# Four small edits to the attention stage: low-rank copies moved on ScalarE, more blank products, V earlier, and scores of two batches as 128-column products

## The chip, the core and the metric

The kernel runs on one core of a Trainium2 chip. A core has five engines that run side by side: TensorE (PE) for matrix products, with its weight loads listed apart as PEld; VectorE (DVE), ScalarE (ACT) and GpSimd (POOL) for elementwise work; and SyncE (SP), which here only issues DMAs. Products write to PSUM, which has banks of 128 rows by 512 fp32 numbers; everything else that is computed lies in SBUF. The metric is the device time of one execution in microseconds, and the kernel before takes 678.25 us (median of 4 runs, 676.69 to 679.31).

## What is computed

A linear attention block with decay feeds a channel mixer with a low-rank token mixing in front. Batch 4, 8 heads, 768 positions, head size 64.

```python
for b in range(nb):                        # blocks of positions
    intra = einsum('bhic,bhjc->bhij', qb, kb) * Dmask      # decay lam^(i-j), j <= i
    intra = einsum('bhij,bhjd->bhid', intra, vb)
    inter = einsum('bhid,bhde->bhie', qb * lam_pow, kv_state)
    out[:, :, sl] = intra + inter
    kv_state = lam_block * kv_state + einsum('bhsd,bhse->bhde', kb * rev_pow, vb)
x = out as (B, S, H*D)                     # 4 x 768 x 512
h = x^T @ U @ V                            # rank 32, over the positions
u = x + h^T
out = u + relu(u @ w_ch1) @ w_ch2          # 512 -> 2048 -> 512
```

U, V, w_ch1 and w_ch2 arrive as 64-bit floats and are turned into fp32 on the chip.

## The kernel before

The attention is cut into 24 steps s of 128 positions, six to a batch. One step has these pieces, each a function of s. `prep` turns q and k of the step with four PE transposes each (L344, banks pq and pk, copied to SBUF by ACT at L347 as qt and kt). `scores` multiplies kt by qt into the two banks pss (L389): for each pair of heads a and each of its two heads x (64 rows of the array each) two products of 64 columns, so 16 products. `masked` multiplies them by the decay mask on DVE (L398, tile sm). `inter` is the carried state's part (L430) and `intra` the step's own (L442); both add into the banks px, which ACT copies to x_nat (L447). `state` makes the new carried state: the product pkv (L407, in the bank pk) and its sum with the faded old state on DVE (L413, L415, tile kv; `fade` on ACT, L381). POOL scales q and k (L372, L361).

An fp32 product shows in the trace as two passes, so 16 products are 32 matmuls and 32 weight loads.

After a batch's six steps `low` multiplies x by U (L457, result pp in the bank of pq), and `low_rows` cuts pp into a high part and a rest: four masks on DVE (L470, tile p_h), two copies of the high part to four-way stacked rows on ACT (L473 h, L474 h2), four differences on DVE (L476, l), and a copy of l on POOL (L479, l2). `mix` multiplies these rows by V's rows v_hl and adds the result to x (L484, L487); `turn` transposes the sum u for the mixer's first product (L501 to L525). p_hl and v_hl lie in one tile, which the profile calls vp.

The order is written out by hand: the list `pieces` (L531 to L547) says which piece follows which, and each engine gets its instructions in that order and runs them in that order. In a step s the pieces are prep(s+1), scale(s+1), then at a batch's first step mix, low and low_rows of the batch before, then intra(s), late, state(s), scores(s+1), inter(s+1), masked(s+1), fade(s+1), aside, turn.

`aside(s)` runs small steps of converting U, V and w_ch1, as the lists at L604 to L608 place them; what they need of ACT is kept back and issued by `late` after the next intra. For V the ten steps are two loads, four conversion steps, the mask with the first two ACT copies (`five`, L576), the difference for one row group on DVE, the last two ACT copies, and the difference for the last row group on POOL. Their places are 0, 0, 3, 3, 4, 4, 5, 5, 5, 5, so that all four ACT copies (L585) come out behind intra of s = 6.

At the start `keep_busy(n)` (L326) issues n products of zeros: one before the product pl, which spreads lam over the rows (L643), and two after it. The first step's q and k are loaded and turned in two halves.

After the attention come the mixer's first product (`hidden`, L695 and L705, whose first units also take the last batch's low, low_rows, mix and turn, by the list `rest` at L749) and its second (`product`, L826 to L830).

Of the kernel before, what the change touches and what calls it, by code (L numbers as in the profile page):

```python
# [8 lines left out]
FP32 = mybir.dt.float32  # L9
# [5 lines left out]
P = 128  # L15
# [3 lines left out]
def kernel(  # L19
# [27 lines left out]
    nc = tc.nc  # L47
# [3 lines left out]
    NT = S // P  # L51
    C = H * D
# [25 lines left out]
    late = []  # L78

    def on_scalar(what):  # L80
        if late and late[0] is None:
            late.append(what)
        else:
            what()
# [12 lines left out]
    def tmp(name):  # L97
        return wconv.tile([P, C], FP32, tag="tmp", bufs=3, name=name)
# [121 lines left out]
    def w1_steps(ft, in_parts=False):  # L220
        def tile_of():
            w1v[ft] = w1_pool.tile([P, 3, C], F32R, tag="w1", name="w1")
            return w1v[ft]

        cols = moe_w_ch1[:, ft * P : (ft + 1) * P].rearrange("(c p) f -> p c f", p=P)
        return split_steps(tile_of, cols, in_parts)
# [13 lines left out]
    def two_banks(name, tag):  # L240
        return psf.tile([P, 2, N], FP32, tag=tag, name=name)

    def one_bank(shape, name, tag):
        return psf.tile(shape, FP32, tag=tag, name=name)
# [11 lines left out]
    def parts(s):  # L256
        return 2 if s == 0 else 1
# [60 lines left out]

    xs = {}
    st = {}
    kv = {}
    half = [slice(0, D), slice(D, P)]

    def keep_busy(n, cols=P):  # L326

        out = one_bank([P, C], "idle", "pq")
        for i in range(n):
            nc.tensor.matmul(  # L330
                out=out[:, 0:cols], lhsT=blank, rhs=blank[:, 0:cols], start=True, stop=True
            )

    qts, kts = {}, {}

    def turn_half(s, a0, name):

        ts, tag = (qts, ("pq", "pt")) if name == "q" else (kts, ("pk", "pu"))
        if a0 == 0:
            ts[s] = att.tile([P, HP, P], FP32, tag=name + "t", bufs=2, name=name + "t")  # L340
        n = HP // parts(s)
        pt = one_bank([P, n, P], "p" + name, tag[a0 > 0])
        for a in range(a0, a0 + n):
            nc.tensor.transpose(  # L344
                out=pt[:, a - a0, :], in_=raw[s, name][:, 2 * a : 2 * a + 2, :], identity=ident
            )
        nc.scalar.copy(ts[s][:, a0 : a0 + n, :], pt)  # L347

    def prep(s):
        for a0 in range(0, HP, HP // parts(s)):  # L350
            for name in "qk":
                turn_half(s, a0, name)
        st[s].update(qt=qts.pop(s), kt=kts.pop(s))
        for name in "qk":
            load_next(name)
# [27 lines left out]
    def scores(s):  # L383
        qt, kt = st[s]["qt"], st[s]["kt"]
        st[s]["pss"] = pss = two_banks("pss", "pss").rearrange("p x (a i) -> p x a i", a=HP)
        for a in range(HP):
            for x in range(2):
                for t in range(2):
                    nc.tensor.matmul(  # L389
                        out=pss[half[t], x, a, :], lhsT=kt[half[x], a, half[t]],  # L390
                        rhs=qt[half[x], a, :], start=True, stop=True,
                    )

# [56 lines left out]
    pps = {}  # L450
# [13 lines left out]
    def low_rows(b):  # L464

        pp, t = pps.pop(b), tmp("p_h")[0:R]
        h, h2, l, l2 = (p_hl[g * R : (g + 1) * R] for g in range(G))
        own = [(slice(g * R, (g + 1) * R), slice(g * P, (g + 1) * P)) for g in range(G)]
        for rows, cols in own:
            nc.vector.tensor_scalar(  # L470
                t[:, cols].bitcast(U32), pp[rows].bitcast(U32), HI, None, ALU.bitwise_and
            )
        nc.scalar.copy(h, t)  # L473
        nc.scalar.copy(h2, t)  # L474
        for rows, cols in own:
            nc.vector.tensor_tensor(  # L476
                out=l[:, cols], in0=pp[rows], in1=t[:, cols], op=ALU.subtract
            )
        nc.gpsimd.tensor_copy(out=l2, in_=l.bitcast(FP32))  # L479

    def mix(s):
        b, c = divmod(s, NT)
# [49 lines left out]
    for s in range(NS):  # L532
        b, c = divmod(s, NT)
        done = s - NT - 1
        more = s + 1 < NS
        step = [("prep", s + 1), ("scale", s + 1)] * more
        step += [("mix", done)] * (0 <= done < NS - NT - 1)
        step += [("low", b - 1)] * (c == 0 and b > 0)
        step += [("low_rows", b - 1)] * (c == 0 and b > 0)
        step += [("intra", s)] + [("late", s)] * (done < 0) + [("state", s)]  # L540
        step += [("turned", done - 1)] * (done > 0) + [("late", s)] * (done >= 0)
        step += [("scores", s + 1)] * more
        step += [("aside", s)] * (done >= 0)
        step += [("inter", s + 1), ("masked", s + 1), ("fade", s + 1)] * more
        step += [("aside", s)] * (done < 0)
        step += [("turn", done)] * (done >= 0 and done // TG < FG)
        pieces += step  # L547
    waiting = {name: list(range(NS)) for name in "qkv"}

    def load_next(name, engine=nc.sync):  # L550
        if waiting[name]:
            load(name, waiting[name].pop(0), engine)


    run = {
        "prep": prep, "fade": fade, "scores": scores, "masked": masked, "inter": inter,
        "intra": intra, "state": state,
        "low": low, "low_rows": low_rows, "mix": mix, "turn": turn,
        "scale": scale, "turned": lambda s: turned.pop(s)(),
    }  # L560
    def v_steps():

        st = {}

        def dst():
            if "v" not in st:
                st["v"] = wconv.tile([P, C], FP32, tag="wf", name="vf")[0 : 2 * R, 0:SH]
            return st["v"]

        def parts(gs):  # L570
            for half in range(2):
                rows, cols = slice(half * R, (half + 1) * R), slice(half * SH, (half + 1) * SH)
                for g in gs:
                    yield v_hl[g * R : (g + 1) * R, cols], rows

        def five():  # L576
            st["t"] = t = wconv.tile([P, C], FP32, tag="wt", name="vt")[0 : 2 * R, 0:SH]
            nc.vector.tensor_scalar(
                t.bitcast(U32), st["v"].bitcast(U32), HI, None, ALU.bitwise_and
            )  # L580
            on_scalar(lambda: high(0))

        def high(g):
            for out, rows in parts((g,)):
                nc.scalar.copy(out, st["t"][rows])  # L585

        def low(g, engine):
            for out, rows in parts((g,)):
                engine.tensor_tensor(
                    out=out, in0=st["v"][rows], in1=st["t"][rows], op=ALU.subtract  # L590
                )

        halves = [moe_V[:, half * SH : (half + 1) * SH] for half in range(2)]
        return weight_steps(dst, halves, SH, 2 * R, in_parts=True) + [
            five, lambda: low(1, nc.vector), lambda: on_scalar(lambda: high(2)),
            lambda: low(3, nc.gpsimd),
        ]
# [5 lines left out]
    side = {}  # L603
    for steps, at in (  # L604
        (u_side, (-1, 1, 1, 2, 2)),
        (v_steps(), (0, 0, 3, 3, 4, 4, 5, 5, 5, 5)),
        (w1_steps(0, True), (3, 4, 5, 6, 8, 9, 10, 11, 12, 13, 14)),
        (w1_steps(1, True), (8, 9, 10, 11, 15, 16, 17, 18, 19, 20, 21)),  # L608
    ):
        assert len(steps) == len(at)  # L610
        for step, n in zip(steps, at):
            side.setdefault(n, []).append(step)
# [15 lines left out]
    blank = x_pool.tile([P, C], FP32, tag="x", name="blank")[:, 0:P]  # L628
# [9 lines left out]
    for name in "qkv":  # L638
        load_next(name)
    make_identity(nc, ident)  # L640
    keep_busy(1)
    pl = one_bank([P, H], "pl", "pt")
    nc.tensor.matmul(out=pl, lhsT=lam_row[:, H:], rhs=lam_row[:, 0:H], start=True, stop=True)  # L643
    keep_busy(2)
    nc.vector.tensor_copy(out=lamb, in_=pl)
    constants()
    powers()
# [92 lines left out]
    def run_units(units, side, every=lambda i: None):  # L740
# [7 lines left out]
    c0, b = NS - NT, B - 1  # L748
    rest = [  # L749
        (0, 4, "enter", None),  # L750
        (0, 4, "turn", c0 - 2), (0, 6, "mix", c0 - 1), (0, 9, "low", b), (0, 14, "low_rows", b),
        (0, 18, "turn", c0 - 1), (0, 22, "mix", c0),
    ]

# [174 lines left out]
```

## Time and profile before

| what | value |
|---|---|
| median of 4 runs | 678.25 us (676.69 to 679.31) |
| profiled execution | 679.33 us, span 677.3 us |
| PE busy | 665.0 us, 98% of the span |
| DVE, ACT, POOL busy | 498.7, 291.6, 116.4 us |
| attention | from 0 to about 125 us |
| first product of the mixer | about 125 to 402 us |
| second product | about 402 to 677 us |
| DMA share, 0 to 44.9 us | 0.90 to 0.96 |

The span runs from the first to the last instruction of the profiled execution. PE's busy share is that of matmuls which are pipelined, with modelled ends. In a row of the timeline a bracket gives the idle time before an instruction and what ended it; "issue" means that the profile shows nothing it waited for. Where several waits end close together, the engine named is the one that came last by the records, and need not be the cause. The mixer's two products run almost without a hole on PE, so the places to look at are those before about 155 us.

### The profile page before, as it was taken

The page shows a single profiled execution, that of the slowest core. Times are in us where ns is not written, and L with a number is a line of the kernel's source. Part 1 is how long each engine was busy: PE and PEld are TensorE (multiplying, and loading weights), DVE is VectorE, ACT ScalarE, POOL GpSimd, SP SyncE. Part 2 cuts the span into 40 slices and gives each one's busy share as a digit, 9 for nine tenths or more (in the row PEclk, how much of TensorE's full clock was granted, in tenths as well). Part 3 has the DMA queues.
Part 4 walks back from the last instruction along what each step waited for, and adds up shares of the span by engine and source line. Part 5 has one row for each costly group of instructions (what it writes and reads, how often), then busy time and mean ns, then how long its engine had stood idle before and what let it go on. Part 6 is the DMA issues. An engine that isn't in the chain of part 4 may idle for free.

```text
span 677.3 us, 13604 instructions
## 1 busy us (share of the span) xinstructions
PE 665.0 (98%) x5312; PEld 543.7 (80%) x5312; DVE 498.7 (74%) x877; ACT 291.6 (43%) x543; POOL 116.4 (17%) x96
## 2 busy tenths in 40 slices
PE   9989999999999999999999999999999999999997
PEld 7878888878888888888888888888888888888885
DVE  4679999776999777777798256786586775865864
ACT  4667768644666444444465131232232322322320
POOL 4456767431000000000000000030030200300300
PEclk9999999999999999999999999999999999999999
DMA  9899894154677655555566999844353363453521
GB/s 214 206 226 227 209 233 129 60 200 161 234 261 254 235 204 201 206 203 203 203 248 252 325 320 388 300 161 162 96 202 109 109 202 94 153 158 93 162 87 63
DMA packets 131777, 131.30 MB, mean 194 GB/s; under 512 B 81346, under 2 KB 89794, under 8 KB 131714
## 3 DMA queue, kind: packets, MB, share of 16 engines
q1 hardware_dynamic: 130656, 130.18, 60.6%
q8 instruction: 42, 0.69, 0.4%
q10 hardware_dynamic: 1058, 0.26, 0.2%
q14 instruction: 21, 0.17, 0.1%
HBM read 80.09 MB, written 50.33 MB: 193 GB/s over the span
## 4 chain that ended last, share of the span: by engine, by line
PE 94%; ACT 2%; DVE 1%; issue 1%; DMA 1%; POOL 0%; ACTq 0%; DVEq 0%
PE pz L695 27%; PE pz L826 13%; PE pz L828 13%; PE pd L705 13%; PE pd L830 13%; PE pss L389 3%; PE px L442 3%; PE put L501 2%; PE pq L344 1%; PE px L430 1%; PE pk L344 1%; PE pkv L407 1%; PE pu L484 1%; PE pp L457 1%; DMA kraw<-in_k_dram 1%
## 5 line engine op out<-in xcount | busy, mean ns | idle before, releaser
L695 PE MATMUL pz<-u_hl,w 128*128 128x512 f32 x768 | 190.7, 398 | 0.2 <-ACT r L701 0.2
L695 PEld LDWEIGHTS pz<-u_hl,w 128*128 128x128 f32 x768 | 143.9, 188 | 35.8 <-ACT r L701 0.9
L826 PE MATMUL pz<-w_hl,m 128*128 128x512 f32 x384 | 151.6, 396 | 0.0
L828 PE MATMUL pz<-w_hl,m 128*128 128x512 f32 x384 | 151.6, 396 | 0.0
L830 PE MATMUL pd<-w_d,m 128*128 128x512 f32 x384 | 150.0, 396 | 0.0
L809 ACT ACTIVATE m<-mt 128x512 fp32r<-128x512 f32 x96 | 60.7, 632 | 195.6 <-PE pd L830 144.5
L810 DVE SCALAR_TENSOR_TENSOR m<-rm,m 128x512 fp32r<-128x512 f32 x96 | 71.5, 746 | 54.1 <-ACT m L809 53.8
L855 POOL TENSOR_TENSOR o<-o,u 128x512 f32<-128x512 f32 x20 | 29.9, 1524 | 447.4 <-DVE o L851 447.4
L710 DVE SCALAR_TENSOR_TENSOR r<-pd,r 128x512 f32<-128x512 f32 x96 | 61.8, 686 | 55.9 <-ACT r L701 45.5
L705 PE MATMUL pd<-u_d,w 128*128 128x512 f32 x384 | 98.2, 397 | 0.0
L826 PEld LDWEIGHTS pz<-w_hl,m 128*128 128x128 f32 x384 | 72.3, 188 | 17.6
L828 PEld LDWEIGHTS pz<-w_hl,m 128*128 128x128 f32 x384 | 72.3, 188 | 17.7
L830 PEld LDWEIGHTS pd<-w_d,m 128*128 128x128 f32 x384 | 72.3, 188 | 17.6
L705 PEld LDWEIGHTS pd<-u_d,w 128*128 128x128 f32 x384 | 72.2, 188 | 17.4
L701 ACT ACTIVATE r<-pz 128x512 f32<-128x512 f32 x96 | 52.0, 593 | 59.1 <-PE pz L695 59.1
L811 DVE SCALAR_TENSOR_TENSOR m<-m 128x512 fp32r<-128x512 f32 x96 | 69.1, 721 | 0.9
L808 DVE TENSOR_SCALAR mt<-rm 128x512 uint32<-128x512 uint32 x96 | 46.1, 481 | 25.1 <-DMA rm<-r_d 24.8
L204 ACT CAST w<-wt 128x512 fp32r<-128x512 f32 x32 | 19.9, 622 | 40.9 <-DVE wt L201 33.7
L398 DVE TENSOR_TENSOR sm<-pss,mask 128x512 f32<-128x512 f32 x48 | 30.8, 682 | 8.0 <-PE pss L389 7.8
L159 ACT ACTIVATE sc<-sc,ends 128x512 f32<-128x512 uint32 x30 | 21.7, 723 | 18.4 <-DVE sc L153 18.4
L372 POOL TENSOR_TENSOR qs<-qt,powq 128x512 f32<-128x512 f32 x20 | 25.8, 1288 | 21.6 <-ACT qt L347 18.6
L442 PEld LDWEIGHTS px<-vraw,sm 128*64 128x64 f32 x768 | 24.5, 138 | 6.0 <-DVE sm L398 2.3
(83 smaller groups left out, 710.6 us busy)
## 6 DMA issues: line engine op xcount, KB each, us to landing
r_d<-r SPq DMA_DIRECT2D x96, 256.0 KB, 2.6
rm<-r_d SPq DMA_DIRECT2D x96, 256.0 KB, 2.7
words<-in_moe_w_ch_dram SPq DMA_DIRECT2D x30, 512.0 KB, 4.5
w_d<-w SPq DMA_DIRECT2D x16, 768.0 KB, 3.3
w_hl<-w_d SPq DMA_DIRECT2D x16, 512.0 KB, 6.2
vraw<-in_v_dram SPq DMA_DIRECT2D x24, 256.0 KB, 4.5
u_d<-x_nat SPq DMA_DIRECT2D x24, 256.0 KB, 3.6
u<-u_d SPq DMA_DIRECT2D x24, 256.0 KB, 4.1
```

Source lines behind the costliest of these rows:

```text
L442: nc.tensor.matmul(out=px[half[t], x, a, :], lhsT=sm[:, x, a, half[t]], rhs=vr[:, 2 * a + x, :], start=(first and a == 0), stop=(a == HP - 1),
L695: nc.tensor.matmul(out=acc[g][0], lhsT=w[:, n, ct, :], rhs=uhl[g][:, n, ct, :], start=(ct == 0 and n == 0), stop=(ct == CT - 1 and n == 1),)
L701: nc.scalar.mul(rs[g], acc[g][0], 1.0 + E)
L705: nc.tensor.matmul(out=acc[g][1], lhsT=w[:, 2, ct, :], rhs=ud[g][:, ct, :], start=(ct == 0), stop=(ct == CT - 1),)
L710: nc.vector.scalar_tensor_tensor(rs[g], acc[g][1], 4096.0, rs[g], ALU.mult, ALU.add)
L808: nc.vector.tensor_scalar(t.bitcast(U32), r.bitcast(U32), HI, None, ALU.bitwise_and)
L809: nc.scalar.activation(out=m[:, 0], in_=t, func=AF.Relu)
L810: nc.vector.scalar_tensor_tensor(m[:, 1], r, 0.0, hi, ALU.max, ALU.subtract)
L811: nc.vector.scalar_tensor_tensor(m[:, 2], hi, E, low, ALU.mult, ALU.subtract)
L826: nc.tensor.matmul(out=pz, lhsT=m[:, 0, cols], rhs=hl[:, 0], start=first, stop=False)
L828: nc.tensor.matmul(out=pz, lhsT=m[:, 1, cols], rhs=hl[:, 1], start=False, stop=end)
L830: nc.tensor.matmul(out=pd, lhsT=m[:, 2, cols], rhs=dd, start=first, stop=end)
```

## The change

Four edits, all in the attention stage and the code around it.

Blank products: `keep_busy` gets two before pl instead of one, three after it instead of two, and the first step gets one behind each half of q, written to the banks pss.

Scores: for s below 12 (the first two batches) one product with 128 columns of kt takes the place of two with 64; for later steps nothing changes.

Low-rank rows: the copies h and h2 leave `low_rows` and come in a piece of their own, `spread`, behind intra (and so behind x's copy); l2 is copied there too, on ACT instead of POOL. In the last batch `spread` follows `low_rows` directly.

V: the mask and all four ACT copies are placed with step 4 instead of 5, so that the copies come out behind intra of s = 5.

```diff
-    def keep_busy(n, cols=P):
+    def keep_busy(n, tag="pq"):
-        out = one_bank([P, C], "idle", "pq")
+        out = one_bank([P, C], "idle", tag) if tag == "pq" else two_banks("idle", tag)[:, 0]
         for i in range(n):
-            nc.tensor.matmul(
-                out=out[:, 0:cols], lhsT=blank, rhs=blank[:, 0:cols], start=True, stop=True
-            )
+            nc.tensor.matmul(out=out[:, 0:P], lhsT=blank, rhs=blank, start=True, stop=True)
...
                 turn_half(s, a0, name)
+                if s == 0 and name == "q":
+                    keep_busy(1, "pss")
...
             for x in range(2):
-                for t in range(2):
+                for rows in half if s >= 2 * NT else [slice(0, P)]:
                     nc.tensor.matmul(
-                        out=pss[half[t], x, a, :], lhsT=kt[half[x], a, half[t]],
+                        out=pss[rows, x, a, :], lhsT=kt[half[x], a, rows],
                         rhs=qt[half[x], a, :], start=True, stop=True,
                     )
...
-        nc.scalar.copy(h, t)
-        nc.scalar.copy(h2, t)
         for rows, cols in own:
             nc.vector.tensor_tensor(
                 out=l[:, cols], in0=pp[rows], in1=t[:, cols], op=ALU.subtract
             )
-        nc.gpsimd.tensor_copy(out=l2, in_=l.bitcast(FP32))
+
+        def spread():
+            nc.scalar.copy(h, t)
+            nc.scalar.copy(h2, t)
+            nc.scalar.copy(l2, l.bitcast(FP32))
+
+        pps[b] = spread
...
-        step += [("intra", s)] + [("late", s)] * (done < 0) + [("state", s)]
+        step += [("intra", s)]
+        step += [("spread", b - 1)] * (c == 0 and b > 0)
+        step += [("late", s)] * (done < 0) + [("state", s)]
...
-        (v_steps(), (0, 0, 3, 3, 4, 4, 5, 5, 5, 5)),
+        (v_steps(), (0, 0, 3, 3, 4, 4, 4, 5, 4, 5)),
...
-    keep_busy(1)
+    keep_busy(2)
     pl = one_bank([P, H], "pl", "pt")
     nc.tensor.matmul(out=pl, lhsT=lam_row[:, H:], rhs=lam_row[:, 0:H], start=True, stop=True)
-    keep_busy(2)
+    keep_busy(3)
...
         (0, 4, "turn", c0 - 2), (0, 6, "mix", c0 - 1), (0, 9, "low", b), (0, 14, "low_rows", b),
+        (0, 14, "spread", b),
```

More of the change, by code (lines that the diff above doesn't have):

```diff
@@ L557 @@
         "intra": intra, "state": state,
-        "low": low, "low_rows": low_rows, "mix": mix, "turn": turn,
+        "low": low, "low_rows": low_rows, "spread": lambda b: pps.pop(b)(), "mix": mix, "turn": turn,
         "scale": scale, "turned": lambda s: turned.pop(s)(),
```

## The prediction

> **What bounds the kernel now.** I read the page's busy shares, then the table of windows, then the timeline wherever TensorE (PE) idles.
>
> ```profile
> PE 665.0 (98%) x5312; PEld 543.7 (80%) x5312; DVE 498.7 (74%) x877; ACT 291.6 (43%) x543; POOL 116.4 (17%) x96
> 9.90:27.90 18.00, 18.00 (x532) 16.66 (x533) 9.81 (x20) 12.59 (x32) 9.59 (x8) 1.00 0.96 220
> 27.90:44.90 17.00, 13.25 (x347) 11.37 (x345) 11.07 (x23) 9.85 (x22) 8.24 (x9) 1.00 0.91 211
> 155.00:402.00 247.00, 247.00 (x1056) 198.55 (x1055) 188.74 (x337) 121.93 (x213) 1.19 (x1) 1.00 0.67 231
> ```
>
> A window's row has its length, the busy time of PE, weight loads, DVE, ACT and POOL, the granted clock, DMA share and GB/s. From 155 us on PE has hardly a hole and the change touches nothing, so a PE that gets there earlier ends the kernel earlier, one for one. Before that PE's holes sum to 6.7 us (from 5.5 us on), 3.75 of them in 27.9 to 44.9.
>
> ```profile
> 6.12 1.99 PE L389 MATMUL pss<-qt,kt 64*64 64x128 f32 x32
> 11.37 1.10 PE L389 MATMUL pss<-qt,kt 64*64 64x128 f32 x32
> 29.75 0.76 PE L389 MATMUL pss<-qt,kt 64*64 64x128 f32 x17 [1.25 <-issue]
> ```
>
> The timeline's columns are start, length, engine, line. The first scores take 1.99 us, the next 1.10: the PE clock opens late; the granted-clock record begins at 9.66 us. At 28.5 us PE stops for 1.25 us inside one stage, where the program has no wait. Packets of the instruction queue (16 KB, 256 instructions) start 0.8 to 1.1 us after PE enters a block at 11.9, 16.3 and 20.5 us, but the one due at 24.8 starts at 27.34. I read the stop as late code, behind loads that keep the DMA engines 96% busy.
>
> ```profile
> 35.54 1.52 PE L457 MATMUL pp<-x_nat,u_w 128*32 128x128 f32 x48 [0.29 <-ACT qt L347]
> 40.27 0.58 ACT L447 COPY x_nat<-px 128x512 f32<-128x512 f32 x1
> 40.75 2.08 ACT L585 CAST vp<-vt 32x384 fp32r<-32x384 f32 x4
> 40.95 0.69 PE L430 MATMUL px<-kv,qs 64*64 64x64 f32 x32 [1.31 <-POOL ks L361]
> 44.28 0.58 ACT L347 COPY kt<-pk 128x512 f32<-128x512 f32 x1
> 44.91 0.69 PE L407 MATMUL pkv<-vraw,ks 128*64 128x64 f32 x16 [0.91 <-ACT kt L347]
> ```
>
> Between the first and second batch ACT is late. The carried-state product (L430) starts 0.07 us after x's copy ends (40.85), which frees its bank px; POOL, the engine named, only ended at the same moment. V's four copies then hold ACT for 2.08 us, kt comes late, and the state product waits 0.91 us for the bank pk.
>
> ```profile
> 72.58 0.42 DVE L413 COPY kv<-pkv 128x256 f32<-128x256 f32 x1
> 72.63 0.58 ACT L447 COPY x_nat<-px 128x512 f32<-128x512 f32 x1
> 73.32 0.30 PE L430 MATMUL px<-kv,qs 64*64 64x64 f32 x5 [0.83 <-POOL vp L479]
> ```
>
> One batch later it is the same, and kv is nearly as late (73.00) as x (73.21).
>
> ```profile
> 85.55 1.01 PEld L442 LDWEIGHTS px<-vraw,sm 128*64 128x64 f32 x32 [0.24 <-DVE ut L506]
> 86.48 0.55 PEld L407 LDWEIGHTS pkv<-vraw,ks 128*64 128x64 f32 x16
> 87.10 0.86 PEld L389 LDWEIGHTS pss<-qt,kt 64*64 64x64 f32 x32
> 87.92 0.61 PEld L430 LDWEIGHTS px<-kv,qs 64*64 64x64 f32 x32
> 88.60 0.20 PEld L501 LDWEIGHTS put<-ident,x_nat 128*128 128x128 f32 x2
> ```
>
> A plain step costs PE start to start: intra 0.93, state 0.62, scores 0.82, inter 0.68 us.
>
> **The change part by part.**
>
> *Blank products, 4 more* (one before pl, one after, one behind each half of q at s = 0). Cold, a 128-column pass takes 0.21 us (two q transposes 3.87 to 4.32 are 0.44) and an fp32 product has two, so each blank costs 0.43. The first ends as lam lands (PE waits 0.20 for it at 2.05), the second fills the hole before q (3.84). The two behind q are on PE's path: k's second half lands at 5.45 and would be turned from 6.0 instead of 5.50, scores start some 0.5 later. Against that, the clock. With blanks until 6.0 I let it open one recording window sooner. Then scores(0) run 6.4 to 7.4, its masking waits for DVE's powers (7.22) and for the scores, prep(1) ends by 8.35, and the first intra starts near 8.8 instead of 9.82: -1.0. If it opens at 9.66 all the same: +0.5. Nearest rows: 1.99 against 1.10 for scores. Behind it loads could bind: q(2) lands at 11.66, 1.2 us ahead of its use at 12.87, so 1.0 still fits. I take -1.0.
>
> The skill's "TensorE: Matmul & The Clock Gate" (Part 1) says that the gate's window runs free of the kernel, so the opening moves from run to run. This trace shows one opening only. By the rule some runs open early already, and half of it, -0.5, would be left in a median.
>
> *Scores in 128-column products, s = 0 to 11* (the condition keeps halves for s >= 12). Per step 8 products instead of 16: 16 fewer passes and 16 fewer loads, 32 of some 240 instructions. Array time: the 32 passes of 64*64 start in fours every 109 ns (8 x 0.109 = 0.87). With 64 rows x 128 columns two tiles fit, 16 passes in twos: 8 x 0.109 again, if the two row halves overlap. No row shows this shape; inter (64*64, four at once) shows that row halves do overlap, the transposes (128*128, one per 109 ns) that whole-array passes don't. Bounds per step: 0 and +0.87. I take 0, since inter shares the row split. What is added for sure is a change of shape between scores and inter in 10 steps. Nearest row: state (128*64) to scores (64*64) opens with 0.10 to 0.15 us more than the passes before it follow each other. Bounds: 0 and 10 x 0.15 = +1.5. In batch 0 intra is released by DVE's masking (26.23, PE at 26.30), which hides most of it, and batch 1 has holes behind two of its five; without these covers it would be +1.5. I charge three steps, +0.3.
>
> The skill's "TensorEngine Tiling (Array Packing)", Key Properties, speaks against this edit: changing the tiling mode, not just the tile, drains the engine. By it all ten steps pay, and the sum below would be 1.2 worse.
>
> *Late code.* A block lasts 256 of 208 instead of 256 of 240 instructions, 0.6 us more at 4.07 us a step. The stop of 1.25 ends between 0 and 1.25 shorter; a block that is consumed 0.6 later also meets another queue. I take -1.25. If a packet is late elsewhere, up to +1.25.
>
> *V sooner.* The mask (DVE, 0.34) goes ahead of masked(6), where DVE is idle (33.0 to 34.29). The four ACT copies go behind x's copy of s = 5, 33.8 to 35.9. Behind them wait qt(7) and kt(7): 36.46 and 36.95 instead of 35.49 and 35.97; the low-rank product needs qt's bank, so its wait grows by 0.97, and intra(6) starts at 38.0 instead of 36.99. But p_h on DVE waited until 37.73 for V's low part anyway, so it slips by 0.3, kv(7) ends at 40.98, inter(7) starts at 41.04 (+0.1). With ACT then free kt(8) ends at 43.7, and the state product follows intra at 43.9 instead of 44.91: -1.0. If qt(7) slips further it is 0.
>
> *Low-rank copies.* On ACT, h and h2 (0.62 each) go behind x, and l2 (0.60 on POOL) joins them as 0.62. POOL's other work stands in the same order and has room. At 72: x ends at 71.6, inter can start at kv + 0.06 = 73.06, -0.25; but te, hi, faded, qt(14), kt(14) slip by 0.4 and the next state product waits until 76.6, where it stood at 76.56. So 0 at both such places (without l2 it would be -0.25 each), and its gain at 41 is in the line above. In the fourth batch l2 ends at 133.5, before pu's 133.66; r (L701) slips 0.6 behind it, hidden by pd products until 134.2, +0.6 if not.
>
> SP issues the same DMAs in the same order.
>
> *Sum:* -1.0 + 0.3 - 1.25 - 1.0 = -2.95 against the profiled 679.33 us (span 677.3 and 2.0 around it): **676.4 us**. That execution is 1.1 above the median of 678.25, so against the median it is -1.85, or -0.27%.
>
> **The rivals.**
> *The code stops are worth more.* The median's own runs spread from 676.69 to 679.31, as stops of 1 to 2.5 us that come and go would make them; seven more code packets fall in batch 1, where the DMA engines are 91 to 92% busy. If the change ends these too, and no shape change shows: 2 us less, 674.4. Against it: this trace has one stop only.
> *The gains are in the best runs already.* Clock early, no stop in half of before's runs, and shape changes paid: V's -1.0, half the clock -0.5, +1.5 less the stop's half -0.6: 677.7.
> *Slower: row halves don't overlap.* Scores then take 16 x 0.109 = 1.74 instead of 0.87 in 12 steps on PE's path: +10.4, 686.8. For it: no row has 64 x 128. It decides against the others once a score stage is over about 1.15 us instead of 0.82 (12 x 0.33 = 3.9, to 0.3% above the median).
> *Slower by lateness:* the blanks delay k and the clock stays (+0.5 for -1.0), qt(7) holds the low-rank product and V gains nothing: 676.4 + 1.5 + 1.0 + 1.2 for the shape changes = 680.1, and some more if the stop stays.
>
> **How the numbers follow.** Forecast 0.45 (own range 675.0 to 677.8, 0.27 of it under 676.2); more code stops ended 0.25; gains present already 0.10; row halves 0.12; lateness 0.08, counted slower with the stop. A measurement of this kernel tells about 0.3% (2.0 us) from no change. Faster by that: 0.27 + 0.25 = 0.52; within: 0.18 + 0.10 = 0.28; slower: 0.20. The range leaves out the row halves and the tail of the first rival: 674.0 to 681.2.
>
> **What would show it.** The granted clock starting near 6.3 and scores(0) at 1.1 us, or not; scores of s < 12 at 0.82 us start to start (1.7 for the rival); inter 0.1 to 0.15 later behind them; no hole marked issue before 45 us; the hole before L457 grown to 1.3 and that before L407 gone; x's copy straight behind intra at 71 us, kv releasing inter. I am wrong if a score stage or a qt copy has become what PE waits for.

## The result and the profile after

The changed kernel takes 677.54 us (median of 52 runs, 676.67 to 678.79) beside 678.89 for the kernel before on the same chip (78 runs, 675.92 to 681.25). The ratio is 0.9982, with an interval of 0.9977 to 0.9988: faster, but by 0.18%, inside the 0.3% that I had set as the bound of a measurable change. Its profiled execution took 677.97 us, span 676.2; the one before took 679.33. The two profiles differ by 1.36 us, the two medians by 1.35, so the profiles can be compared step by step. (Of the 1.36, 1.14 lie in the span, 677.3 to 676.2; the rest lies outside it.)

The page's busy shares, and two rows of the table of windows (length, busy time and instructions of PE, weight loads, DVE, ACT, POOL, granted clock, DMA share, GB/s):

```profile
PE 667.0 (99%) x5128; PEld 545.8 (81%) x5128; DVE 496.5 (73%) x877; ACT 294.1 (43%) x547; POOL 113.4 (17%) x92
9.90:27.90 18.00, 17.90 (x428) 15.91 (x427) 9.32 (x21) 12.06 (x32) 8.28 (x7) 1.00 1.01 228
27.90:44.90 17.00, 15.31 (x367) 13.66 (x363) 10.88 (x25) 11.95 (x25) 9.61 (x9) 1.00 0.98 232
```

PE has 184 instructions fewer, and yet 2.0 us more of busy time. Between 27.9 and 44.9 us it is busy for 15.31 instead of 13.25 us, since holes have closed. What follows is the start of intra(s), the pace of the kernel, read from the timelines of both:

| intra of step | before, us | after, us | after minus before |
|---|---|---|---|
| 0 | 9.82 | 10.16 | +0.34 |
| 1 | 13.89 | 14.77 | +0.88 |
| 4 | 26.30 | 27.64 | +1.34 |
| 5 | 32.03 | 31.93 | -0.10 |
| 6 | 36.99 | 37.79 | +0.80 |
| 8 | 48.72 | 47.88 | -0.84 |
| 12 | 69.83 | 69.10 | -0.73 |
| 15 | 85.55 | 84.33 | -1.22 |
| 23 | 124.30 | 123.02 | -1.28 |

The kernel loses 1.3 us up to step 4, wins it back in step 4 alone, loses 0.9, wins 1.6, and is 1.2 to 1.3 us ahead from step 15 on. The timeline of after (start, length, engine, line, operation, tiles) has the first loss and a plain step of batch 0, one in which PE has no hole:

```profile
7.20 2.00 PE L390 MATMUL pss<-qt,kt 64*128 64x128 f32 x16
...
10.16 1.47 PE L443 MATMUL px<-vraw,sm 128*64 128x64 f32 x32
...
23.35 1.15 PE L443 MATMUL px<-vraw,sm 128*64 128x64 f32 x32
24.33 0.64 PE L408 MATMUL pkv<-vraw,ks 128*64 128x64 f32 x16
24.89 1.16 PE L390 MATMUL pss<-qt,kt 64*128 64x128 f32 x16
25.99 0.69 PE L431 MATMUL px<-kv,qs 64*64 64x64 f32 x32
26.61 0.66 PE L343 MATMUL pq<-ident,qraw 128*128 128x128 f32 x4
```

The first scores start 1.08 us later than before and still take 2.00 us: the blanks delayed them and the clock was not yet open. From score start to inter start it is now 1.10 us (before 0.93), from there to the transposes 0.62 (before 0.57): the plain step grew from 4.07 to 4.29 us. The same stages in the timeline of before:

```profile
23.77 1.10 PE L389 MATMUL pss<-qt,kt 64*64 64x128 f32 x32
24.70 0.64 PE L430 MATMUL px<-kv,qs 64*64 64x64 f32 x32
25.27 0.66 PE L344 MATMUL pq<-ident,qraw 128*128 128x128 f32 x4
```

Single score passes of after start in pairs every 112 ns, so the two row halves do run at once. The stop of 1.25 us with issue as its reason is gone; no PE hole of after has that reason. The change of batches:

```profile
33.61 2.07 ACT L592 CAST vp<-vt 32x384 fp32r<-32x384 f32 x4
35.70 0.58 ACT L346 COPY qt<-pq 128x512 f32<-128x512 f32 x1
36.34 1.52 PE L458 MATMUL pp<-x_nat,u_w 128*32 128x128 f32 x48 [1.15 <-ACT qt L346]
40.47 0.42 DVE L414 COPY kv<-pkv 128x256 f32<-128x256 f32 x1
41.04 0.69 PE L431 MATMUL px<-kv,qs 64*64 64x64 f32 x32 [0.54 <-DVE kv L414]
43.91 0.64 PE L408 MATMUL pkv<-vraw,ks 128*64 128x64 f32 x16
```

V's copies now stand ahead of qt: the low-rank product waits 1.15 us instead of 0.29, inter 0.54 instead of 1.31, and the state product no longer 0.91.

### The profile page after: what moved, and what is told of

The parts are those of the page before. It is cut to its first block, busy times and chain, and to the rows that moved or that the text cites. A ratio compares the mean times of both kernels' runs of the same rounds, so it can differ in the third digit from the quotient of the medians.

```text
span 676.2 us, 13225 instructions
## 1 busy us (share of the span) xinstructions
PE 667.0 (99%) x5128; PEld 545.8 (81%) x5128; DVE 496.5 (73%) x877; ACT 294.1 (43%) x547; POOL 113.4 (17%) x92
## 4 chain that ended last, share of the span: by engine, by line
PE 95%; DVE 2%; ACT 1%; issue 1%; DVEq 0%; ACTq 0%
PE pz L702 27%; PE pz L834 13%; PE pz L836 13%; PE pd L712 13%; PE pd L838 13%; PE px L443 3%; PE pss L390 3%; PE put L506 2%; PE pq L343 2%; PE px L431 2%; PE pk L343 1%; PE pkv L408 1%; PE pp L458 1%; PE pu L489 1%; PE idle L331 1%
```

## The experiments

My theory after the result was this. V's step works as worked out. The 128-column scores cost 0.22 us in each step that no wait hides, and take away stops in which PE waits for its instructions. The blanks bring nothing. The rivals: the stops have nothing to do with the number of instructions, the gain is V's alone, or the clock does open sooner with blanks.

All ratios are to the kernel before, timed on the same chip together with that row's kernel. "Stops" are PE holes of the profiled execution that have issue as their reason; "clock" is where its record of the granted clock begins.

| kernel | median (lowest to highest), runs | ratio, interval | stops, us | clock, us | intra(0), us |
|---|---|---|---|---|---|
| before | 678.89 (675.92 to 681.25), 78 | 1 | 1.25, 0.18 | 9.66 | 9.82 |
| after | 677.54 (676.67 to 678.79), 52 | 0.9982, 0.9977 to 0.9988 | none | 8.99 | 10.16 |
| scores_only | 678.38 (678.12 to 679.31), 12 | 0.9994, 0.9984 to 1.0004 | none | 9.05 | 9.66 |
| v_only | 678.61 (676.01 to 679.76), 12 | 0.9986, 0.9972 to 0.9999 | none | 9.84 | 10.02 |
| blanks_only | 678.54 (676.99 to 680.28), 12 | 0.9990, 0.9976 to 1.0003 | 0.16, 0.41, 0.64 | 8.71 | 9.97 |
| spread_only | 678.52 (676.56 to 681.15), 12 | 0.9992, 0.9977 to 1.0007 | 0.76, 0.43, 0.39, 0.59 | 10.43 | 10.51 |
| no_blanks | 677.80 (677.17 to 678.83), 11 | 0.9984, 0.9975 to 0.9993 | none | 11.15 | 10.58 |
| no_scores | 677.14 (676.06 to 679.74), 10 | 0.9980, 0.9969 to 0.9990 | 1.20 | 7.64 | 9.45 |
| code_pressure | 683.48 (682.73 to 686.25), 6 | 1.0075, 1.0060 to 1.0091 | 0.44, 0.19, 0.43, 0.89, 0.70, 0.74 | 9.50 | 10.16 |
| v_spread_pool | 677.47 (676.05 to 680.20), 12 | 0.9980, 0.9966 to 0.9994 | 0.80, 0.50 | 10.11 | 10.50 |
| inter128 | 679.13 (678.55 to 679.86), 12 | 1.0004, 0.9991 to 1.0017 | none | 7.16 | 9.40 |
| fitted | 678.31 (677.61 to 678.66), 12 | 0.9993, 0.9980 to 1.0006 | none | 10.24 | 10.79 |
| combo_b1 | 676.10 (675.39 to 676.62), 6 | 0.9962, 0.9948 to 0.9977 | none | 7.87 | 9.56 |
| combo_s3 | 677.82 (676.37 to 679.34), 12 | 0.9985, 0.9970 to 0.9999 | 0.85 | 7.85 | 9.55 |

**One part at a time.** Four kernels, each the kernel before with one part of the change's diff.

*scores_only*:

```
-                for t in range(2):
+                for rows in half if s >= 2 * NT else [slice(0, P)]:
```

> The kernel before with 128-column scores for s below 12 and nothing else. Theory (late code): the score stage, first load to inter's first load, takes 1.09 us instead of 0.82 and a step of the first batch 0.22 more, so a fixed cost of about 1.0 us in four to five steps of the first batch and almost none in the second, against stops of PE's code that come and go in the kernel before (one of 1.25 us in its profile) and should be gone; together a median within 0.7 us of the kernel before, a smaller spread of the runs, and no hole marked issue before 45 us. Rival (the stops have nothing to do with the number of instructions): the fixed cost alone, 1.0 to 1.5 us slower, and the spread of the runs as before.

*v_only*:

```
-        (v_steps(), (0, 0, 3, 3, 4, 4, 5, 5, 5, 5)),
+        (v_steps(), (0, 0, 3, 3, 4, 4, 4, 5, 4, 5)),
```

> The kernel before with V's mask and ACT copies one step sooner and nothing else. Theory: the one edit that shortens PE's path in every run; the low-rank product of the first batch waits about 0.9 us more for qt, the hole of 0.91 us before the second step's state product is gone; but without the low-rank copies behind x, x's copy still comes late and inter waits for it. Net 0.7 to 1.0 us faster, with the spread of the kernel before. Rival: the low-rank product's longer wait eats it, 0 to 0.3 us.

*blanks_only*, the two calls of `keep_busy` and the one behind q's halves:

```
+                if s == 0 and name == "q":
+                    keep_busy(1, "pss")
...
-    keep_busy(1)
+    keep_busy(2)
...
-    keep_busy(2)
+    keep_busy(3)
```

> The kernel before with four more blank products and nothing else. Theory: each of the two blanks behind q costs 0.43 us at half rate on PE's path, and the granted clock opens near 9 us as without them, so the first intra starts 0.3 to 0.6 us later, 0.2 to 0.5 us slower in the median. Rival (the forecast): the clock opens one window of 3.4 us sooner in most runs, the first scores take 1.1 us, and it is 0.5 to 1.0 us faster.

*spread_only*, h, h2 and l2 put behind x's copy on ACT:

```
-        nc.scalar.copy(h, t)
-        nc.scalar.copy(h2, t)
...
-        nc.gpsimd.tensor_copy(out=l2, in_=l.bitcast(FP32))
+        def spread():
+            nc.scalar.copy(h, t)
+            nc.scalar.copy(h2, t)
+            nc.scalar.copy(l2, l.bitcast(FP32))
```

> The kernel before with the low-rank copies behind x's copy on ACT and nothing else. Theory: inter of s = 7, 13 and 19 starts behind kv instead of x, 0.2 us sooner, and at 13 and 19 the third copy on ACT takes most of it back; at 7, V's copies now stand another 0.6 us later on ACT, so that the state product's wait of 0.91 us there grows to about 1.3. Net 0 to 0.4 us slower. Rival: the copies matter by themselves, 0.5 us faster.

The four medians lie 0.9 to 1.1 us below the kernel before (679.49 on that chip; by the ratios it is 0.4 to 1.0), with intervals that overlap and all but one of which hold 1, so the medians don't rank the parts. blanks_only and spread_only, which I had put at up to 0.5 us slower, came out where their rivals had them; but the kernel before itself came to 679.49 and, in the runs beside inter128 and fitted, to 678.78 on that same chip, so neither is decided. Two things can be read. The runs of scores_only lie within 1.2 us, those of the other three spread over 3.3 to 4.6. And v_only's profiled execution, which met no stop, took 676.59 us; in it the low-rank product waits 1.06 us and the state product not at all, as in after, while scores_only keeps the old waits:

```profile
34.92 1.52 PE L457 MATMUL pp<-x_nat,u_w 128*32 128x128 f32 x48 [1.06 <-ACT qt L347]
42.59 0.64 PE L407 MATMUL pkv<-vraw,ks 128*64 128x64 f32 x16
```

The timeline of spread_only has four stops, the last three beyond the first two batches:

```profile
29.87 0.76 PE L389 MATMUL pss<-qt,kt 64*64 64x128 f32 x17 [0.76 <-issue]
...
74.33 0.62 PE L430 MATMUL px<-kv,qs 64*64 64x64 f32 x26 [0.43 <-issue]
...
89.36 0.57 PE L430 MATMUL px<-kv,qs 64*64 64x64 f32 x21 [0.39 <-issue]
...
106.03 0.50 PE L430 MATMUL px<-kv,qs 64*64 64x64 f32 x17 [0.59 <-issue]
```

A stop splits a group in the middle, where the program has no wait, and its place and length differ from kernel to kernel.

**The change without one part.** *no_blanks* is the changed kernel with the four blanks taken out again (the diff of blanks_only backwards); *no_scores* has 64-column scores in all steps:

> The changed kernel without its four more blank products; scores, V and low-rank copies as in the change. Theory (the blanks only delay k's turn): the first scores start near 6.2 us again instead of 7.20, the first intra near 9.8 instead of 10.16, the clock record still begins between 8.7 and 10.4 us; median 0.3 to 0.5 us below the changed kernel's 677.54, so 677.0 to 677.3, and its runs stay within 2 us of each other. Rival (the blanks open the clock sooner, in runs that no profile caught): 0.5 to 1.0 above the changed kernel's, 678.0 to 678.5.

> The changed kernel with all scores in 64-column products, as before the change; blanks, V and low-rank copies as in the change. Theory (the 128-column products cost some 0.2 us a step in batch 0 and take away the code stops): the fastest runs are 0.6 to 1.0 us faster than the changed kernel's fastest 676.67, so 675.7 to 676.1; the slowest come up to 679 to 680 again, the runs spread over some 4 us, and the median is 677.5 to 678.2. Rival (late code is a matter of chance and not of the number of TensorE instructions): no wider spread than the changed kernel's 2.1 us and a median of 676.5 to 677.0.

no_blanks gives 0.9984 against 0.9982 with blanks: on the median the blanks are worth nothing that shows. Its profile is not what I expected either: k landed late (PE waits 0.64 us for it, as it does for 0.26 to 1.00 in six of the seven traces with the old blanks), scores start at 6.67, the clock record at 11.15 and intra(0) at 10.58, later than after's:

```profile
5.16 0.69 PE L344 MATMUL pk<-ident,kraw 128*128 128x128 f32 x2 [0.64 <-DMA kraw<-in_k_dram]
```

In no_scores the spread came back (3.7 us against 2.1), the fastest run (on another chip) is 0.6 below after's, as the theory had it; the median, 677.14, is a little better than I had put it, and its ratio the same as after's. So the score edit is worth nothing that shows on the median: about what it saves in stops it pays in every run. The timeline of no_scores has both, a clock that opened during the first scores and a stop:

```profile
7.20 1.29 PE L389 MATMUL pss<-qt,kt 64*64 64x128 f32 x32
9.45 1.50 PE L442 MATMUL px<-vraw,sm 128*64 128x64 f32 x32
...
33.90 0.43 PE L389 MATMUL pss<-qt,kt 64*64 64x128 f32 x3 [1.20 <-issue]
```

**More instructions for the same columns.** *code_pressure* is the kernel before with each score product of s < 12 cut in two:

```
+                    for cols in half if s < 2 * NT else [slice(0, P)]:
                         nc.tensor.matmul(
-                            out=pss[half[t], x, a, :], lhsT=kt[half[x], a, half[t]],
-                            rhs=qt[half[x], a, :], start=True, stop=True,
+                            out=pss[half[t], x, a, cols], lhsT=kt[half[x], a, half[t]],
+                            rhs=qt[half[x], a, cols], start=True, stop=True,
```

> The kernel before with each score product of s = 0 to 11 split into two of 64 moving columns: 64 passes a step instead of 32 for the same columns, so 32 more instructions for the matmul queue and 32 more weight loads, and nearly no more array time where a pass is as long as its columns. Theory (late code behind a busy DMA): a block of 256 instructions is used up 0.7 to 0.9 us sooner, so stops with issue as their reason stand at most of the block boundaries between 16 and 70 us, 0.3 to 1.5 us each, and the median is 3 to 9 us above the kernel before's. Rival (code is fetched in time, the one stop of the profile before was something else): no more than one such hole, and a score stage of the same length or up to 0.4 us longer in the 12 steps; median 0 to 2 us above in batch 0, 5 at the most, with the increase lying in the score stages and not in holes.

It is 4.4 us slower than the kernel before. Its page and its timeline:

```profile
PE 667.8 (98%) x5696; PEld 546.4 (80%) x5696; DVE 498.3 (73%) x877; ACT 291.8 (43%) x543; POOL 116.3 (17%) x96
```

```profile
21.48 0.64 PE L390 MATMUL pss<-qt,kt 64*64 64x64 f32 x26 [0.44 <-issue]
...
25.83 1.03 PE L390 MATMUL pss<-qt,kt 64*64 64x64 f32 x52 [0.19 <-issue]
...
30.03 0.27 PE L443 MATMUL px<-vraw,sm 128*64 128x64 f32 x1 [0.43 <-issue]
...
34.71 1.04 PE L443 MATMUL px<-vraw,sm 128*64 128x64 f32 x28 [0.89 <-issue]
...
43.18 0.45 PE L390 MATMUL pss<-qt,kt 64*64 64x64 f32 x6 [0.70 <-issue]
...
61.95 0.44 PE L502 MATMUL put<-ident,x_nat 128*128 128x128 f32 x2 [0.74 <-issue]
```

Six stops, 3.39 us in all, where the kernel before has 1.43 in two. That the stops grow with PE's instruction count is shown. The rest of the loss is not stops: its plain step takes 4.29 us, 0.22 more, which I had put at nearly nothing. So the rival that puts the increase into the score stages is half right. That the instructions are late because the DMA engines are busy (99 and 92% busy in the two windows of its table) was argued from packets of the instruction queue; no run took the load away, and it stays open.

That the stops are late code can be read from the traces themselves. Count PE's instructions (weight loads, matmuls and semaphore instructions) in order of their start: in all 19 stops of the 14 traces the first instruction behind the stop has a number of the form 194 + 256 k, so each stop stands at the edge of a block of 256 instructions. And each ends 1.15 to 1.54 us after a packet of 16 KB on the instruction queue has landed. In the five kernels with 128-column scores in both batches the packet landed 1.5 to 5.6 us ahead of every such edge up to 126 us. A block lasts longer there: in batch 0, free of stops, 3.9 us in code_pressure, 4.2 to 4.4 before, and 4.6 to 5.8 in after. Smaller delays at these edges don't show as holes: the passes of v_only at 71.10 us and of combo_b1 at 19.46 start 0.20 us behind the ones before them. So "none" in the table means no hole, not that no run and no edge lost time.

**V and the low-rank copies alone, l2 left on POOL.** *v_spread_pool* is v_only with spread_only's diff, but l2's line stays as it was:

> The kernel before with V's copies sooner and h and h2 put behind x's copy, l2 left on GpSimd, no more blanks, scores in 64-column products. Theory: V's 0.9 us at the state product of s = 7, and 0.1 to 0.25 at each of the two later batch changes because l2 takes no ScalarE time there: 1.1 to 1.4 us below the kernel before in fastest and in median run (677.5 to 678.2 by the shared 678.9 to 679.5), with the same spread of some 4 us. Rival (gains before 155 us are lost in a wait for loads): no more than V alone, 0.9 below.

1.6 us below the kernel before, interval 0.9966 to 0.9994: as far as the whole change, without more blanks and without 128-column scores, though with two stops in its profile. The intervals are too wide to tell V alone (0.9986) from V with the copies.

**Is the 0.22 us a change of shape?** *inter128* gives inter the shape of the scores:

```
-                for t in range(2):
+                for rows in half if s >= 2 * NT else [slice(0, P)]:
                     nc.tensor.matmul(
-                        out=px[half[t], x, a, :], lhsT=st[s]["qs"][half[x], a, half[t]],
+                        out=px[rows, x, a, :], lhsT=st[s]["qs"][half[x], a, rows],
```

> The changed kernel with the carried-state product (inter) of s = 1 to 11 also in products of 64 rows by 128 columns, 16 passes instead of 32, so that scores and inter have one shape. Theory (the 0.22 us a step are the change from 64x128 to 64x64 products): scores and inter together take 1.50 to 1.55 us again instead of 1.72, the plain step of batch 0 is 4.07 to 4.15 us instead of 4.29, intra(5) starts 0.7 to 1.1 us sooner relative to intra(0), and the median lies 0.5 to 1.1 us below the changed kernel's, ratio to before 0.9966 to 0.9975. Rival (the longer weight loads of 128 columns cost it, 214 against 160 ns a group): inter becomes as long as scores or longer, the step is 4.29 or more, and the ratio is 0.998 or above.

The rival holds: the plain step is 4.51 us, and the ratio is 0.0022 above after's, some 1.5 us, in another set of runs. The timeline of inter128, with the plain step's scores and inter:

```profile
7.20 1.25 PE L390 MATMUL pss<-qt,kt 64*128 64x128 f32 x16
...
24.78 1.16 PE L390 MATMUL pss<-qt,kt 64*128 64x128 f32 x16
25.78 1.01 PE L431 MATMUL px<-kv,qs 64*128 64x64 f32 x16
26.71 0.66 PE L343 MATMUL pq<-ident,qraw 128*128 128x128 f32 x4
```

From scores to inter it is 1.00 us here, 1.10 in after and 0.93 before. So, as far as one such run can tell, 0.10 of the 0.22 goes with the change of shape between the two stages, 0.07 stays with 128-column scores when there is none, and 0.05 lies at inter's end. Inter itself takes 0.93 us instead of 0.57: its passes are 64 columns long, its weights 128, and 16 passes of a 64-column product came no faster than 16 passes of a 128-column one (pairs every 112 ns in both). That the weights set this pace is my reading; no run has weights of another length there. In neither stage did halving the passes make the stage itself shorter: scores, with 128 moving columns, lost the 0.22 us, inter, with 64, another 0.22.

**Blanks cut to the holes.** *fitted* is no_blanks with these:

```
     keep_busy(1)
+    keep_busy(1, D)
     pl = one_bank([P, H], "pl", "pt")
...
     keep_busy(2)
+    keep_busy(1, D // 2)
...
+                if (s, a0, name) == (0, 0, "q"):
+                    keep_busy(1, tag="pss")
```

> The changed kernel with the blank products cut to the holes: one of 64 columns ahead of pl (the hole of 0.20 us at 2.05), one of 32 ahead of q (0.10 at 3.86), one of 128 behind the first half of q (0 to 1.0 us for k's load), none behind the second half. Theory (the clock opens earlier when TensorE has had no hole, and the change's blanks lost that again by delaying q by 0.6 us and the scores by 1.1): q is turned at 3.85 to 3.95, the scores start at 6.2 to 6.6, the granted clock begins at 7.6 to 9.0 and not at 9.0 to 11.2, the first intra starts at 9.0 to 9.6 instead of 10.16 and 10.58 (without blanks); median 0.4 to 1.0 us below 677.5. Rival (the opening falls where it likes): it lies between 9.0 and 11.2, the first intra at 9.8 to 10.6, and the median within 0.3 us of the kernel without blanks.

A miss in its design. The first products in its timeline:

```profile
1.05 1.54 PE L330 MATMUL idle<-blank 128*128 128x128 f32 x4 [1.05 <-DVE blank L637]
2.52 0.59 PE L652 MATMUL pl<-lam_row 1*128 1x8 f32 x2
3.04 1.92 PE L330 MATMUL idle<-blank 128*128 128x128 f32 x6
5.06 0.66 PE L344 MATMUL pq<-ident,qraw 128*128 128x128 f32 x2
```

pl comes at 2.52 instead of 2.05 and q at 5.06 instead of 3.86. A further call of `keep_busy` takes its bank anew, and its first pass started 0.48 us behind the pass before (1.42 to 1.90) instead of the 0.21 between passes of one call. So the short blanks cost more than the long ones. On the clock the run speaks for the rival: PE has no hole over 0.11 us until the scores, as with the change's blanks, and yet the record begins at 10.24. Its median is 0.5 us above that of no_blanks, more than either side had put.

**128-column scores only where they are hidden.** Both kernels are the changed one with l2 left on POOL, and the condition of the score loop altered, *combo_b1*:

```
-                for rows in half if s >= 2 * NT else [slice(0, P)]:
+                for rows in [slice(0, P)] if NT <= s < 2 * NT else half:
```

and *combo_s3* with `3 <= s` in place of `NT <= s`.

> The changed kernel with l2's copy left on GpSimd and 128-column scores in the second batch alone (s = 6 to 11), 64-column ones in the first. Theory (128-column scores cost 0.22 us a step in the first batch, where no wait hides it, and 0.1 in all in the second, where they take the code stops away): plain steps of batch 0 at 4.07 us, no hole with issue as its reason behind 37 us, one or none before; the fastest runs 675.5 to 676.2, the median 676.6 to 677.2, ratio 0.9968 to 0.9978. Rival (the stops fall in the first batch, so they all stay): a spread of some 4 us and a median of 677.1 to 677.6, as with 64 columns everywhere.

> The same with 128-column scores in s = 3 to 11. Theory (the stops begin at 20 us or later, and three steps of the first batch pay 0.22): first steps at 4.07, those behind s = 2 at 4.29; no hole with issue as its reason; the runs within 2 us of each other, fastest 676.0 to 676.7, median 676.6 to 677.2. Rival (every 64-column step brings the stop nearer wherever it falls): a stop of 0.3 to 1.3 us between 16 and 35 us in the profile and a spread of 3 us or more.

combo_b1 is the fastest kernel of the study: 0.9962, interval 0.9948 to 0.9977, 2.8 us below the kernel before, from only six runs, and the end of its interval touches the beginning of after's. Windows and timeline of it:

```profile
9.90:27.90 18.00, 17.87 (x524) 16.60 (x524) 9.74 (x21) 12.27 (x32) 9.54 (x8) 1.00 0.93 212
27.90:44.90 17.00, 15.31 (x383) 13.47 (x380) 11.52 (x25) 11.72 (x26) 9.90 (x10) 1.00 0.96 222
...
9.56 1.50 PE L443 MATMUL px<-vraw,sm 128*64 128x64 f32 x32
...
36.50 1.15 PE L443 MATMUL px<-vraw,sm 128*64 128x64 f32 x32
```

Intra(0) starts 0.60 us and intra(6) 1.29 us sooner than in after; what lies between, 0.7 us, is the 64-column steps of batch 0 without a stop. It came out 0.5 us below the theory's median; the rival's wide spread did not come. combo_s3 shows the limit of it: its runs spread over 3.0 us, as its rival had it, its median is 0.6 above the theory's, and its stop came where neither had put one, at 91.7 us, in a step whose scores are in 64-column products in every kernel here:

```profile
90.36 0.51 PE L431 MATMUL px<-kv,qs 64*64 64x64 f32 x20
91.72 0.45 PE L431 MATMUL px<-kv,qs 64*64 64x64 f32 x12 [0.85 <-issue]
```

Why after's and combo_b1's blocks arrived in time there and this one's did not is open. That 128 columns in the second batch alone keep the stops away in every run is not shown either: six runs within 1.2 us speak for it, and a different set of six may not; combo_s3, with more 128-column steps, has the wide spread.

## Why the prediction was right or wrong

The range (674.0 to 681.2) held the time. The likeliest value, 676.4, was 1.1 us too low: 0.6 because 78 runs put the kernel before at 678.89 where the four that I had gave 678.25, and 0.5 because the gain was 1.35 and not 1.85. Faster by over 0.3%, to which I gave 0.52, did not come. That a range of 7.2 us held says little for the sum: profile against profile it forecast -2.95, and -1.36 came. Of its four terms one had the wrong sign and one was four times too small. That it did not end further off is luck in part, since the stop of before was worth 1.67 instead of 1.25 and -0.33 came unforeseen. The steps, in the order of the sum, each against the profile of before:

- *Blanks, -1.0.* This failed first, and in its sign: +0.34 at intra(0) in the profile of after. The step had two errors. The early blanks were put at nothing, "fills the hole before q"; the holes are 0.20 and 0.10 us, a blank is 0.43, and q went from 3.87 to 4.48. So scores start at 7.20 instead of the 6.4 that I let them. And the clock did not open near 6.3. Yet it may answer to the blanks: its record begins between 7.16 and 8.99 us in the six traces with the change's blanks (mean 8.04) and between 9.05 and 11.15 in the seven with the old ones (mean 9.96). What in them moves it is not shown: six of the seven wait for k, but fitted, without such a hole, begins at 10.24. Intra(0) starts at 9.68 and at 10.18 on the mean, -0.5, but with the new blanks it then waits inside for the second half of DVE's masking (1.47 us long in after, 1.15 before). Taking the start of intra(1) less a plain step, the means are 10.02 and 10.21: -0.2 is left, which fits with the medians of after and no_blanks. After's own trace has the latest opening of its six.
- *The clock page.* What "TensorE: Matmul & The Clock Gate" (Part 1) of the Trainium skill says of a window that runs free of the kernel agrees with an opening that moves over 1.8 us among traces with the same new blanks, and over 2.1 with the old. Its -0.5 was nearer to the -0.2 than my -1.0.
- *Scores, +0.3.* The overlap was right (row halves overlap, pairs every 112 ns, so the rival with 686.8 fell), and the price was off. It costs 0.22 us a step in five steps of batch 0, where I had let DVE's masking hide it, and 0.1 in all in batch 1: +1.2. The failing words are "in batch 0 intra is released by DVE's masking (26.23, PE at 26.30), which hides most of it": PE reaches the next intra 0.22 later and so does everything.
- *The tiling page.* By Key Properties of "TensorEngine Tiling (Array Packing)" all ten steps were to pay, +1.5; measured +1.2, so its sum was nearer than mine. But inter128, which has no such change between the two stages, puts the change of shape at 0.10 of the 0.22.
- *Late code, -1.25.* Right in its mechanism, as the block edges and code_pressure show, and too small for this trace: the step with the stop took 5.74 us, 1.67 above a plain one. The edges that I had counted (11.9, 16.3, 20.5, 24.8) stand 0.8 to 1.0 us too late by those of the stops; from the latter the late packet started 3.4 us behind its edge, the three before it 1.6 to 2.1. For the median it is worth less, since a stop does not come in every run.
- *V sooner, -1.0.* Right, wait by wait, and a quarter smaller in sum: the low-rank product's wait grew by 0.86 (0.97 predicted), inter came at 41.04 as predicted, released by kv, and the state product at 43.91 (43.9). From intra(5) to intra(8) it is 15.95 us instead of 16.69: -0.74.
- *Low-rank copies, 0.* Right within 0.2 us: intra(12) to intra(13) is 0.16 shorter and the next step 0.12 longer; at the next change of batches 0.20 and 0.13. With l2 on POOL, as in combo_b1, the second part does not come back (4.73 instead of 4.86 and 4.87). In the fourth batch r slips by 0.6 as worked out, but its cover is not complete: at pd (133.94 us before, 132.61 after) the lead is still 1.33, at the pu behind it (134.87 and 133.71) 1.16; combo_b1, with l2 on POOL, keeps its 2.86.

The ledger closes: +0.34 (start), +1.24 (0.54, 0.04, 0.22, 0.22 and 0.22 in steps 0 to 4; the first has 0.32 of the wait inside intra(0), and in the second the kernel before lost 0.18 of its own), -1.67 (stop), -0.74 (V), +0.10 (scores in batch 1), -0.16 (copies), -0.33 between intra(13) and intra(15), where before had a stop of 0.18 and a wait of 0.24 for DVE's ut, and -0.06 up to intra(23): -1.28. I had no term for the -0.33. The fourth batch's loss takes it to the span's -1.14.

So blanks and scores, together forecast at -0.7, cost some 1.7 us in this trace, and the stop that the scores ended gave 1.67 back. On the median, where neither edit shows anything, V and the copies of h and h2 alone reach what the whole change reaches; how the gain divides between these two is open.

## What to carry to other kernels

A product with half the passes saves instructions, and need not save time: here two stages became slower by it. Compare the columns of the weights with those that move, and look for the stage behind it that changes shape. Read the spread of a kernel's runs before costing a hole that its trace shows once; a hole marked issue inside a group of products is such a case. Count the instructions up to it: if such holes are whole blocks of 256 apart, the code came late, and fewer instructions per us help. Blanks cost what they are longer than the hole that they fill (two of 0.43 us in holes of 0.20 and 0.10 delayed q by 0.61), and more calls of shorter ones can cost more still.

## What was unexpected of the hardware

- 64 passes of 64 moving columns for the scores, for the same columns, made a plain step 0.22 us longer (4.29 instead of 4.07 with 32 passes of 128), as much as the 16 passes of 64 x 128 did.
- 16 passes of 64 x 128 with 64 moving columns took 0.93 us, 32 of 64 x 64 took 0.57: the larger products were the slower ones.
- The clock's opening moved from 7.16 to 11.15 us over 14 traces, and no stop in PE's instructions occurred in the five with 128-column scores in both first batches, while five of the six with 64 columns throughout (code_pressure aside) had one to four.
- All 19 stops stand whole blocks of 256 instructions apart in PE's own count, and each ends 1.15 to 1.54 us after a 16 KB packet of the instruction queue landed.
- A first pass in a bank just given up started 0.48 us after the pass before, at the closed clock, instead of 0.21.
